# Three later forward transforms at 2.5 classic steps a pair, and 512-token chunks from token 4096, in a fused Fourier-mix and feed-forward kernel

## The chip, the cores and the metric

The kernel runs on one core of a Trainium2 chip. The metric is device time in microseconds (us) of one execution: the median of three runs before is 1351.38 us (1350.46 to 1352.64).

## What is computed

```python
def _attn_ref(x, w_r, w_i, b_r, b_i):            # x: (4, 3008, 256)
    X = np.fft.rfft(x, axis=1)
    Yr = X.real @ w_r - X.imag @ w_i + b_r
    Yi = X.real @ w_i + X.imag @ w_r + b_i
    Yr = np.sign(Yr) * np.maximum(np.abs(Yr) - 0.01, 0.0)
    Yi = np.sign(Yi) * np.maximum(np.abs(Yi) - 0.01, 0.0)
    return np.fft.irfft(Yr + 1j * Yi, n=3008, axis=1)

def _moe_ref(x, w_in, w_out, alpha):             # x: (12032, 256), w_in: (256, 2048)
    h = x @ w_in
    g = np.maximum(h, 0.0) + alpha * np.minimum(h, 0.0)
    return g @ w_out                             # (12032, 256)
```

The first function's result, 4 batches of 3008 tokens, is the second one's input: 12032 tokens. Everything is float32.

## The kernel before

**The transform.** A batch's 3008 points are 47 times 64. Stage a (`a_load`, `a_split`, `a_mm`, `a_evac`, 16 groups a batch) is the 47-point part. Its result goes to DRAM and comes back regrouped as 12 *pairs* (`b_load`). For each pair, stage b (`b_mm`, `b_evac`, `b_evac2`) is the 64-point part; stage m is the complex mix as three real products (`m_mm` two of them, `m_mm2` the third), then the additions, bias and soft shrink on VectorE (`m_part`, in eight parts n = 0 to 7: part 0 adds the bias into a tile Yc, line 526; parts 1 to 4 are four 64-row *quarter additions* from Yc and the third product into a tile Yt, line 532; part 5 bounds, lines 505 and 506; part 6 subtracts, line 511; part 7 makes the low half of a split, line 520); and stage c (`c_mm`, `c_evac`) begins the inverse transform and stores to DRAM. Yt and Yc have one buffer each. Stage d (`d_load`, then `d_step` or `s_dmm`) is the last 47-point part; a call gives 376 tokens, split by `split` (lines 139 and 142) on ScalarE and VectorE into a high and a low half, the feed-forward's input.

**The feed-forward, in two forms.** All its products are of split operands (high times high, high times low, low times high: three matmuls for one).
- *Classic chunks* have 384 tokens (the first of each half of the 16 has 256). A classic *step* is one chunk and one of 16 blocks of 128 hidden units: `l1_step` runs six matmuls into a `ps_h` tile (line 686), ScalarE makes relu(-h) (line 692), VectorE scales and adds (line 693), ScalarE copies the high half gh (line 697), VectorE or GpSimd makes the low half gl (line 698); `l2_step`, three steps later, runs the second layer's matmuls (lines 723 to 725). `CC = 12` chunks are classic, 192 steps in all.
- *512-token chunks* take the rest, from token `T0`. For two hidden blocks at once (a *pair t*, 8 a chunk) `s_l1` runs 12 matmuls (line 791), and `s_sums` and `s_l2` multiply with seven products instead of eight (pair t = 1 is plain, with eight; lines 892 to 894). At a chunk's end `s_out` combines the sums (VectorE, eight operations, lines 920 to 927) and, two pairs later, `s_turn` transposes them (line 936). The last chunk, here called the *rest*, has `ZC` tokens and is plain (`z_parts`, lines 837 and 838; `z_l2`, lines 855 to 857; its copies and stores, lines 862 to 865). `T0` is 4480, so there are 14 full chunks and a rest of 384 tokens.

**What orders the work.** The first batch's transform runs ahead of all this. The three later ones are woven into the classic steps by a table written out by hand: `at(i, fn, ...)` puts a call at the end of step i, and `when=mid` puts it inside step i, between the step's scaling and its gh on the engines' queues. Each engine works in that order. Batch b's pair q has its stage b at step `BO[b] + BP * q`, and its other parts at fixed distances from it: `m_mm` 2 steps later, `m_mm2` 4, the eight parts of `m_part` 3 to 6 (`MP`), `c_mm` 8, `b_load` 4 earlier. Stage a's groups follow `AO[b]`, two in three steps. `d_step` of chunk g of a batch is three steps ahead of its first use.

**Buffers.** The tiles `ps_a`, `ps_b`, `ps_m`, `ps_m1`, `ps_c` and `ps_d` share one PSUM pool of three (`ps_f`), in which the 512-token chunks also hold one accumulator and the rest holds its own. `ps_h` and `ps_o` have two buffers each. DMA: loads and stores go over SyncE's queue (SPq); the last stores alternate over SyncE's and ScalarE's queue (ACTq).

The placing lines:

```python
for q in range(NPAIR if b + 1 < B else 0):
    i = BO[b + 1] + BP * q
    at(i, b_mm, b + 1, q)
    at(i + MM, m_mm, b + 1, q)
    at(i + M2, m_mm2, b + 1, q, when=mid)
    for n, k in enumerate(MP):
        at(i + k, m_part, b + 1, q, n, when=mid)
    at(i + CM, c_mm, b + 1, q)
```

Of the kernel before, what the change touches and what calls it, by code (L numbers as in the profile page):

```python
# [9 lines left out]
F32 = mybir.dt.float32  # L10
# [83 lines left out]
def fft_mix_moe(ctx, tc, x, w_r, w_i, b_r, b_i, w_in, w_out, alpha, la, rb, lc, rd, lf, cf, sel, out):  # L94
    nc = tc.nc
    B, S, C = x.shape
# [10 lines left out]
    TC = 384  # L107
    assert NC * TC - 128 == NC * TOK

    CC = 12  # L110
    SC = 512

    def head(c):
        return 128 - (TC - TOK) * (c % NC) if c % NC else 0

    def size(c):
        return TC if c % NC else TC - 128

    T0 = (CC // NC) * NC * TOK + TC * (CC % NC) - (128 if CC % NC else 0)
    NS2 = -(-(B * S - T0) // SC)  # L120
# [4 lines left out]
    work = ctx.enter_context(tc.tile_pool(name="work", bufs=2))  # L125
# [7 lines left out]
    def f(t):  # L133
        return t.bitcast(F32)
# [275 lines left out]
    bt, xs, xe, yc, ys = {}, {}, {}, {}, {}  # L410
# [94 lines left out]
    def m_bound(t, c):  # L505
        V.tensor_scalar(out=c, in0=t, scalar1=-LAM, scalar2=LAM, op0=ALU.max, op1=ALU.min)

    def m_less(b, q, t, c):
        hi = work.tile([128, 2, C], F32R, tag="Yh", name="Yh")
        lo = work.tile([128, 2, C], F32R, tag="Yl", name="Yl")  # L510
        V.tensor_tensor(out=t, in0=t, in1=c, op=ALU.subtract)
        ys[b, q] = hi, lo, t
# [5 lines left out]
    def m_evac2(b, q):  # L518
        hi, lo, t = ys[b, q]
        V.tensor_tensor(out=lo, in0=t, in1=f(hi), op=ALU.subtract)  # L520

    def m_part(b, q, n):
        if n == 0:
            t = work.tile([128, 2, C], F32, tag="Yt", name="Yt", bufs=1)
            c = work.tile([128, 2, C], F32, tag="Yc", name="Yc", bufs=1)
            V.tensor_tensor(out=c, in0=pm.pop((b, q)), in1=bias[0], op=ALU.add)
            yc[b, q] = t, c
        elif n < 5:

            i, s = divmod(n - 1, 2)  # L530
            t, c = yc[b, q]
            V.tensor_tensor(out=t[64 * i:64 * i + 64, s], in0=p1[b, q][64 * s:64 * s + 64],
                            in1=c[64 * s:64 * s + 64, i], op=ALU.add)
        elif n == 5:
            del p1[b, q]
            m_bound(*yc[b, q])
        elif n == 6:
            m_less(b, q, *yc.pop((b, q)))
        else:
            m_evac2(b, q)  # L540
# [43 lines left out]
    def d_open(c):  # L584
# [3 lines left out]
        if head(c):  # L588
            for t, src in zip((hi, lo), heads.pop(c)):
                if c < CC:  # L590
                    t, src = t[:, :, 0:head(c)], f(src)[:, :, 0:head(c)]
# [8 lines left out]
    def d_step(b, g):  # L600
        t = zt.pop((b, g))
        c = NCH * b + g
        assert c < CC
        n0 = (size(c) - head(c)) // CH
# [20 lines left out]
    def s_open(n):  # L625
        yt[CC + n] = [work.tile([128, CT, SC], F32R, tag=tag, name=tag) for tag in ("yh", "yl")]

# [13 lines left out]
    def s_dpart(dg, n):  # L641
        parts = []
        for k, n0, n1, a, z in s_parts(dg):
            if k == n:
                for ct in range(CT):
                    ps = ds[dg][ct][:, :, n0:n1]
                    ys = [y[:, ct] for y in yt[CC + n]]
                    if n == NS2 - 1:
# [132 lines left out]
    def s_l1(n, t):  # L781
        yh, yl = yt[CC + n]
        w1 = SC if n < NS2 - 1 else ZC
        q = work.tile([128, 2, SC], F32, tag="xt", name="sq")[:, :, 0:w1]
        for j in range(2):
            m = 2 * t + j
            ps = ps_h.tile([128, SC], F32, tag="h", name="ps_h")[:, 0:w1]
            k = 0
            for ct in range(CT):
                for w, a in ((0, yh), (0, yl), (1, yh)):  # L790
                    PE.matmul(ps, wi_h[m // FH][:, w, ct, 128 * (m % FH):128 * (m % FH) + 128], a[:, ct, 0:w1],  # L791
                              start=(k == 0), stop=(k == 3 * CT - 1))
                    k += 1
            A.activation(out=q[:, j], in_=ps, func=AF.Relu, scale=-1.0)  # L794
            V.scalar_tensor_tensor(out=q[:, j], in0=q[:, j], scalar=beta_s[:, m:m + 1], in1=ps,  # L795
                                   op0=ALU.mult, op1=ALU.add)
        sq[n, t] = q
# [160 lines left out]
    ES = [1, 1, 1, 1, 1, 1, 1, 1, 1, 0, 1, 0, 0, 0, 0, 0]  # L958
    LOS = [0, 1, 0, 0, 1, 1, 0, 1, 1, 0, 1, 1, 0, 1, 0, 0, 1, 1, 0, 0, 1, 0, 1, 1, 1, 1, 1, 0, 1, 1, 0, 1, 1, 0, 1, 1, 0, 1, 1, 0, 1, 1, 0, 1, 1, 0, 1, 1]
    DS = 3  # L960
    AO = {2: 58, 3: 95}
    BO = {1: 49, 2: 86, 3: 123}
    BP = 3
    SLAG = 2
    PLAIN = (1,)
    MP = [3, 4, 4, 4, 4, 5, 5, 6]
# [21 lines left out]
    with tc.manual_schedule():  # L988
# [100 lines left out]
        def at(i, fn, *args, when=todo):  # L1089
            when.setdefault(i, []).append((fn, args))  # L1090
# [9 lines left out]
        for b in range(B):  # L1100
            s0 = b * per
            for g in range(J if b == 0 else 0, min(NCH, CC - NCH * b)):
                i = s0 + g * FT
                at(i - 8, d_load, b, g)
                at(i - 4 if i == J * FT else i - FT + 1, d_open, NCH * b + g)
                if b == 0 and g == J:
                    at(i - DS, d_step, b, g)
                else:
                    at(i - 3, d_step, b, g)
            if b == 0:  # L1110
                for g in range(FILL, NG):
                    i = 6 * (g - FILL) + 9
                    if g % 2 == 0:
                        at(i - 8, a_load, 1, g // 2)
                    at(i, a_mm, 1, g)
                    at(i, a_evac, 1, g)
            else:
                for g in range(NG if b + 1 < B else 0):
                    i = AO[b + 1] + 3 * g // 2
                    if g % 2 == 0:  # L1120
                        at(i - 5, a_load, b + 1, g // 2)
                    at(i - 2, a_split, b + 1, g)
                    at(i, a_mm, b + 1, g)
                    at(i, a_evac, b + 1, g)
            for q in range(NPAIR if b + 1 < B else 0):
                i = BO[b + 1] + BP * q
                at(i - BL, b_load, b + 1, q)
                at(i, b_mm, b + 1, q)
                at(i, b_evac, b + 1, q)
                at(i, b_evac2, b + 1, q)  # L1130
# [4 lines that stand above are left out]
                at(i + MP[6], m_evac1, b + 1, q)  # L1135
                at(i + CM, c_mm, b + 1, q)
                at(i + CM, c_evac, b + 1, q)
# [4 lines left out]
        i = NS - 26  # L1142
# [55 lines left out]
        for k in range(len(spairs) + SLAG):  # L1198
# [9 lines left out]
            if k >= SLAG:  # L1208
                n, t = spairs[k - SLAG]
# [43 lines left out]
```

## Time and profile before

| | |
|---|---|
| median of three runs | 1351.38 us (1350.46 to 1352.64) |
| the profiled execution | 1351.47 us |
| its span in the trace | 1349.7 us |
| TensorE busy | 1334.4 us (99%), 9200 matmuls |
| VectorE busy | 1035.8 us (77%) |
| ScalarE busy | 760.9 us (56%) |
| GpSimd busy | 379.0 us (28%) |
| granted TensorE clock | 1.00 (mean of the execution) |

Engines are PE (TensorE; PEld is its weight load), DVE (VectorE), ACT (ScalarE), POOL (GpSimd) and SP (SyncE). A releaser is what ended an engine's idle time. The chain is the run of work that ended last, followed back from the last instruction. The stages of the span: the first batch's transform to about 202 us, classic steps to about 680 us, 512-token chunks to 1311 us, then the rest and the last stores.

### The profile page before, as it was taken

Reading aid. Unit: us, or ns where it says so; the run is one execution under the profiler, and the core shown is the slowest. Engines: PE = TensorE matmul, PEld = TensorE weight load, DVE = VectorE, ACT = ScalarE, POOL = GpSimd, SP = SyncE. Lnnn points to the kernel's source line nnn. Section 1 sums busy time; section 2 is a strip of 40 time slices with the busy share of each in tenths; the row PEclk is TensorE's granted clock in tenths of the full one; section 3 lists DMA queues with packets and bytes.
Section 4 is the critical chain, followed back from the end, with each engine's and each line's share of the span. In section 5 each row is a group of like instructions: output and inputs, shape, how many; then the busy total and the mean of one; then the engine's idle time right before and its main releaser. Section 6 shows DMA issues by size and latency. Waiting matters only on the chain.

```text
span 1349.7 us, 25116 instructions
## 1 busy us (share of the span) xinstructions
PE 1334.4 (99%) x9200; PEld 1250.5 (93%) x9200; DVE 1035.8 (77%) x1934; ACT 760.9 (56%) x1527; POOL 379.0 (28%) x403
## 2 busy tenths in 40 slices
PE   8999999999999999999999999999999999999998
PEld 5979999999999999999999999999999999999998
DVE  2767856776777777776778888888888888888885
ACT  3566655665565555555555555655555556555553
POOL 4854742222221222222121211121112112221222
PEclk9999999999999999999999999999999999999999
DMA  9964223342333312111110110111011101110001
GB/s 244 252 197 136 81 95 105 109 136 72 98 113 114 113 52 79 52 58 41 35 36 2 40 28 5 36 28 28 7 34 28 29 7 34 28 28 9 20 17 28
DMA packets 88117, 89.64 MB, mean 66 GB/s; under 512 B 42317, under 2 KB 70448, under 8 KB 87995
## 3 DMA queue, kind: packets, MB, share of 16 engines
q1 hardware_dynamic: 79700, 77.02, 20.0%
q0 software_dynamic: 5168, 8.02, 2.3%
q10 hardware_dynamic: 3127, 3.01, 0.7%
q8 instruction: 72, 1.18, 0.4%
q14 instruction: 50, 0.41, 0.1%
HBM read 50.49 MB, written 34.34 MB: 63 GB/s over the span
## 4 chain that ended last, share of the span: by engine, by line
PE 90%; DMA 3%; DVE 2%; issue 1%; ACT 1%; SPq 1%; POOL 0%; ACTq 0%; DVEq 0%; POOLq 0%
PE ps_h L791 24%; PE ps_h L686 14%; PE ps_m L488 6%; PE ps_o L893 6%; PE ps_o L894 6%; PE ps_o L892 6%; PE ps_d L617 4%; PE ps_o L725 3%; PE ps_o L724 3%; PE ps_o L723 3%; PE ps_b L428 2%; PE o_last L724 1%; PE o_last L725 1%; PE o_last L723 1%; PE o_last L892 1%; PE o_last L893 1%
## 5 line engine op out<-in xcount | busy, mean ns | idle before, releaser
L791 PE MATMUL ps_h<-yh,w 128*128 128x512 f32 (+1 forms) x960 | 315.6, 390 | 0.0
L830 POOL TENSOR_TENSOR l<-t,h 128x512 fp32r<-128x512 f32 x98 | 127.0, 1296 | 496.5 <-ACT h L828 456.6
L791 PEld LDWEIGHTS ps_h<-yh,w 128*128 128x128 f32 x960 | 180.0, 188 | 33.2
L795 DVE SCALAR_TENSOR_TENSOR sq<-sq,beta_s,ps_h 128x512 f32<-128x512 f32 (+1 forms) x240 | 168.0, 733 | 55.0 <-ACT sq L794 54.2
L686 PE MATMUL ps_h<-yh,w 128*128 128x384 f32 (+1 forms) x704 | 206.8, 336 | 0.9 <-DVE q L693 0.9
L791 PE MATMUL ps_h<-yl,w 128*128 128x512 f32 (+1 forms) x480 | 186.3, 388 | 0.0
L693 DVE SCALAR_TENSOR_TENSOR q<-q,beta_s,ps_h 128x384 f32<-128x384 f32 (+1 forms) x192 | 115.5, 602 | 85.3 <-ACT q L692 83.5
L697 ACT ACTIVATE gh<-q 128x384 fp32r<-128x384 f32 (+1 forms) x192 | 99.1, 516 | 144.5 <-DVE q L693 143.5
L698 POOL TENSOR_TENSOR gl<-q,gh 128x384 fp32r<-128x384 f32 (+1 forms) x90 | 96.6, 1074 | 263.2 <-ACT gh L697 256.4
L810 ACT ACTIVATE dh<-sq 128x768 fp32r<-128x768 f32 x112 | 94.7, 846 | 117.9 <-DVE sq L795 75.2
L794 ACT ACTIVATE sq<-ps_h 128x512 f32<-128x512 f32 (+1 forms) x240 | 133.1, 586 | 27.5 <-PE ps_h L791 23.1
L686 PEld LDWEIGHTS ps_h<-yh,w 128*128 128x128 f32 x704 | 129.4, 189 | 3.8 <-issue 0.8
L828 ACT ACTIVATE h<-t 128x512 fp32r<-128x512 f32 x98 | 62.0, 633 | 105.0 <-DVE t L826 101.7
L686 PE MATMUL ps_h<-yl,w 128*128 128x384 f32 (+1 forms) x352 | 116.5, 331 | 0.0
L692 ACT ACTIVATE q<-ps_h 128x384 f32<-128x384 f32 (+1 forms) x192 | 91.7, 478 | 42.5 <-PE ps_h L686 41.0
L725 PE MATMUL ps_o<-w,gl 128*128 128x256 f32 x384 | 108.0, 281 | 1.7 <-POOL gl L698 1.7
L724 PE MATMUL ps_o<-w,gh 128*128 128x256 f32 x384 | 107.8, 281 | 0.0
L723 PE MATMUL ps_o<-w,gh 128*128 128x256 f32 x384 | 107.7, 281 | 0.0
L791 PEld LDWEIGHTS ps_h<-yl,w 128*128 128x128 f32 x480 | 90.6, 189 | 13.6
L825 DVE TENSOR_TENSOR dl<-sq,dh 128x768 fp32r<-128x768 f32 x98 | 93.5, 954 | 3.8 <-ACT dh L810 3.8
L894 PE MATMUL ps_o<-l,sw_a 128*128 128x256 f32 x294 | 82.0, 279 | 0.0
L892 PE MATMUL ps_o<-h,sw_a 128*128 128x256 f32 x294 | 81.9, 279 | 0.0
(214 smaller groups left out, 3620.2 us busy)
## 6 DMA issues: line engine op xcount, KB each, us to landing
zt<-zd SPq DMA_DIRECT2D x32, 384.0 KB
zd<-zst SPq DMA_DIRECT2D x37, 256.0 KB
ad<-ast SPq DMA_DIRECT2D x48, 192.0 KB
bt<-ad SPq DMA_DIRECT2D x72, 128.0 KB
xt<-in_x SPq DMA_DIRECT2D x21, 320.0 KB
out<-oT SPq DMA_DIRECT2D x152, 32.0 KB
cw_s<-in_moe_w_in SPq DMA_DIRECT2D x8, 512.0 KB
cw_s<-in_moe_w_out SPq DMA_DIRECT2D x8, 512.0 KB
```

Source lines behind the costliest of these rows:

```text
L686: PE.matmul(ps, wi_h[m // FH][:, w, ct, 128 * (m % FH):128 * (m % FH) + 128], a[:, ct, 0:n], start=(k == 0), stop=(k == 3 * CT - 1))
L693: V.scalar_tensor_tensor(out=q, in0=q, scalar=beta_s[:, m:m + 1], in1=ps, op0=ALU.mult, op1=ALU.add)
L697: A.activation(out=hi, in_=q, func=AF.Copy)
L723: PE.matmul(a, hi[:, t], w[:, 0], start=(i, k) in first, stop=False)
L724: PE.matmul(a, hi[:, t], w[:, 1], start=False, stop=False)
L725: PE.matmul(a, lo[:, t], w[:, 0], start=False, stop=(i, k) in last)
L791: PE.matmul(ps, wi_h[m // FH][:, w, ct, 128 * (m % FH):128 * (m % FH) + 128], a[:, ct, 0:w1], start=(k == 0), stop=(k == 3 * CT - 1))
L794: A.activation(out=q[:, j], in_=ps, func=AF.Relu, scale=-1.0)
L795: V.scalar_tensor_tensor(out=q[:, j], in0=q[:, j], scalar=beta_s[:, m:m + 1], in1=ps, op0=ALU.mult, op1=ALU.add)
L830: G.tensor_tensor(out=l24, in0=t24, in1=f(h24), op=ALU.subtract)
L892: PE.matmul(o, wh, gh, start=first, stop=False)
L894: PE.matmul(o, wh, gl, start=False, stop=last)
```

## The change

Three numbers of the order change, and one tile of `m_part` is taken later.

```diff
-    CC = 12
+    CC = 11
...
     def m_part(b, q, n):
         if n == 0:
-            t = work.tile([128, 2, C], F32, tag="Yt", name="Yt", bufs=1)
             c = work.tile([128, 2, C], F32, tag="Yc", name="Yc", bufs=1)
             V.tensor_tensor(out=c, in0=pm.pop((b, q)), in1=bias[0], op=ALU.add)
-            yc[b, q] = t, c
+            yc[b, q] = [c]
         elif n < 5:
 
             i, s = divmod(n - 1, 2)
+            if n == 1:
+                yc[b, q].insert(0, work.tile([128, 2, C], F32, tag="Yt", name="Yt", bufs=1))
             t, c = yc[b, q]
...
-    AO = {2: 58, 3: 95}
-    BO = {1: 49, 2: 86, 3: 123}
-    BP = 3
+    AO = {2: 50, 3: 80}
+    BO = {1: 49, 2: 79, 3: 109}
...
-                i = BO[b + 1] + BP * q
+                i = BO[b + 1] + 5 * q // 2
```

One chunk fewer is classic: 176 classic steps instead of 192. `T0` follows: 4096, with 15 full 512-token chunks instead of 14, and a rest of 256 tokens instead of 384. A transform's pairs are 2 and 3 steps apart in turn (six gaps of 2 and five of 3) instead of 3. From `m_part` on, line numbers are higher by one.

Three places in the engines' orders show what moves. The first is ScalarE in the last transform, near classic step 130: `Xh` is the copy of one pair's stage b, and each `q` and `gh` belong to one classic step. Before:

```order
L442 ACTIVATE Xh<-ps_b 128x2x4x64
L457 ACTIVATE sm<-ps_b 128x2x2x64
L692 ACTIVATE q<-ps_h 128x384
L697 ACTIVATE gh<-q 128x384
L692 ACTIVATE q<-ps_h 128x384
L697 ACTIVATE gh<-q 128x384
L567 ACTIVATE zst<-ps_c 128x512
L516 ACTIVATE Yh<-Yt 128x512
L692 ACTIVATE q<-ps_h 128x384
L697 ACTIVATE gh<-q 128x384
L442 ACTIVATE Xh<-ps_b 128x2x4x64
```

After, between two pairs that are two steps apart:

```order
L442 ACTIVATE Xh<-ps_b 128x2x4x64
L457 ACTIVATE sm<-ps_b 128x2x2x64
L693 ACTIVATE q<-ps_h 128x384
L698 ACTIVATE gh<-q 128x384
L693 ACTIVATE q<-ps_h 128x384
L698 ACTIVATE gh<-q 128x384
L516 ACTIVATE Yh<-Yt 128x512
L442 ACTIVATE Xh<-ps_b 128x2x4x64
```

Between two `Xh` there were three classic steps; here there are two.

The second place is VectorE at the stage-d call for classic chunk 7 (step 109 in both): `yl` and `hl` are the low halves of its split, which read the `ps_d` tiles last; `Yc` and `Yt` are parts of `m_part`. Before:

```order
L693 SCALAR_TENSOR_TENSOR q<-q,beta_s,ps_h 128x384
L506 TENSOR_SCALAR Yc<-Yt 128x512
L511 TENSOR_TENSOR Yt<-Yt,Yc 128x512
L698 TENSOR_TENSOR gl<-q,gh 128x384
L142 TENSOR_TENSOR yl<-ps_d,yh 128x312 x2
L142 TENSOR_TENSOR hl<-ps_d,hh 128x64 x2
L142 TENSOR_TENSOR xl<-xt,xh 94x512
```

After:

```order
L694 SCALAR_TENSOR_TENSOR q<-q,beta_s,ps_h 128x384
L506 TENSOR_SCALAR Yc<-Yt 128x512
L511 TENSOR_TENSOR Yt<-Yt,Yc 128x512
L525 TENSOR_TENSOR Yc<-ps_m,bias 128x512
L699 TENSOR_TENSOR gl<-q,gh 128x384
L142 TENSOR_TENSOR yl<-ps_d,yh 128x312 x2
L142 TENSOR_TENSOR hl<-ps_d,hh 128x64 x2
L448 TENSOR_TENSOR Xl<-ps_b,Xh 128x2x4x64
L458 TENSOR_TENSOR sm<-ps_b,sm 128x2x2x64
```

The next pair's bias addition (line 525) now stands between the subtraction of the pair before it and the splits.

The third place is VectorE at the start of the rest: the last row of `s_out` of the last full chunk, then the rest's first three pairs (`zg` is a low half, line 795 is the scaling), then the first two transposes of `s_turn`. Before:

```order
L927 TENSOR_TENSOR c_16203<-su 128x256
L838 TENSOR_TENSOR zg<-sq,zg 128x384
L795 SCALAR_TENSOR_TENSOR sq<-sq,beta_s,ps_h 128x384 x2
L838 TENSOR_TENSOR zg<-sq,zg 128x384
L795 SCALAR_TENSOR_TENSOR sq<-sq,beta_s,ps_h 128x384 x2
L838 TENSOR_TENSOR zg<-sq,zg 128x384
L936 STREAM_TRANSPOSE oT<-c_16202 128x256
```

After:

```order
L928 TENSOR_TENSOR c_16329<-su 128x256
L839 TENSOR_TENSOR zg<-sq,zg 128x256
L796 SCALAR_TENSOR_TENSOR sq<-sq,beta_s,ps_h 128x256 x2
L839 TENSOR_TENSOR zg<-sq,zg 128x256
L796 SCALAR_TENSOR_TENSOR sq<-sq,beta_s,ps_h 128x256 x2
L839 TENSOR_TENSOR zg<-sq,zg 128x256
L937 STREAM_TRANSPOSE oT<-c_16328 128x256
```

The order is the same; the rest's own rows are 256 columns wide instead of 384, and those of `s_out` and `s_turn` are as they were.

## Rows read from the trace of the kernel before

**Rows 1.** The page: busy time of each engine; the chain's shares by engine.
```profile
PE 1334.4 (99%) x9200; PEld 1250.5 (93%) x9200; DVE 1035.8 (77%) x1934; ACT 760.9 (56%) x1527; POOL 379.0 (28%) x403
...
PE 90%; DMA 3%; DVE 2%; issue 1%; ACT 1%; SPq 1%; POOL 0%; ACTq 0%; DVEq 0%; POOLq 0%
```

**Rows 2.** The waits of PE: tile, line, releaser; total us, count, mean us.
```profile
PE ps_m L488 <- DVE hl L142: 0.5, 1, 0.5
...
PE ps_a L392 <- DVE hl L142: 0.3, 1, 0.3
```

**Rows 3.** Windows: us; PE, PEld, DVE, ACT, POOL busy; PEclk, DMA share, GB/s.
```profile
232.00:328.40 96.40, 96.08 (x700) 92.99 (x699) 73.17 (x140) 59.87 (x124) 24.54 (x31) 1.00 0.36 107
467.70:618.00 150.30, 150.30 (x1150) 150.30 (x1149) 109.03 (x216) 77.29 (x160) 41.00 (x55) 1.00 0.19 61
683.60:1311.00 627.40, 627.40 (x4052) 572.35 (x4051) 538.37 (x1016) 364.78 (x706) 128.91 (x100) 1.00 0.09 24
```

**Rows 4.** The chain in classic steps: start us, us, engine, tile, line, count.
```profile
646.43 1.04 PE ps_h L686 x6
648.54 1.04 PE ps_h L686 x6
```

**Rows 5.** The chain in the first 512-token chunk, first layer of four pairs.
```profile
736.67 2.75 PE ps_h L791 x12
741.90 2.75 PE ps_h L791 x12
747.52 2.75 PE ps_h L791 x12
```

**Rows 6.** The chain in the rest of 384 tokens, two pairs.
```profile
1318.75 0.12 PE ps_o L855
...
1319.11 2.08 PE ps_h L791 x12
...
1323.35 2.08 PE ps_h L791 x12
```

**Rows 7.** Lines by form, DVE: shapes, count, busy us, mean ns, idle before, releaser.
```profile
L693 DVE SCALAR_TENSOR_TENSOR q<-q,beta_s,ps_h 128x384 f32<-128x384 f32 x176 | 107.9, 613 | 82.4 <-ACT q L692 80.7
...
L511 DVE TENSOR_TENSOR Yt<-Yt,Yc 128x512 f32<-128x512 f32 x36 | 25.8, 716 | 1.2
L526 DVE TENSOR_TENSOR Yc<-ps_m,bias 128x512 f32<-128x512 f32 x36 | 24.6, 683 | 0.0
...
L693 DVE SCALAR_TENSOR_TENSOR q<-q,beta_s,ps_h 128x256 f32<-128x256 f32 x16 | 7.6, 475 | 2.8 <-ACT q L692 2.8
```

**Rows 8.** Timeline at the stage-d call of chunk 7: start, us; [idle before, releaser].
```profile
428.49 1.92 PE L617 MATMUL ps_d<-rd_s,zt 96*128 96x94 f32 x16
...
431.31 0.21 DVE L142 TENSOR_TENSOR hl<-ps_d,hh 128x64 fp32r<-128x64 f32 x1
...
431.67 0.71 PE L488 MATMUL ps_m<-ws_s,Xh 128*128 128x256 f32 x4 [0.53 <-DVE hl L142]
```

**Rows 9.** Timeline of DVE in the rest.
```profile
1317.01 0.41 DVE L927 TENSOR_TENSOR c<-su 128x256 f32<-128x256 f32 x1
...
1317.81 1.13 DVE L795 SCALAR_TENSOR_TENSOR sq<-sq,beta_s,ps_h 128x384 f32<-128x384 f32 x2
...
1324.86 1.41 DVE L936 STREAM_TRANSPOSE oT<-c 128x256 f32<-128x256 f32 x4
1326.20 1.09 DVE L795 SCALAR_TENSOR_TENSOR sq<-sq,beta_s,ps_h 128x384 f32<-128x384 f32 x2
```

**Rows 10.** Timeline in a transform: POOL and DVE side by side.
```profile
486.70 0.93 POOL L460 TENSOR_TENSOR Xl<-sm,Xh 128x256 fp32r<-128x256 f32 x1
...
487.06 1.11 DVE L511 TENSOR_TENSOR Yt<-Yt,Yc 128x512 f32<-128x512 f32 x1
```

**Rows 11.** Timeline of the last stores: ScalarE's queue and ScalarE.
```profile
1344.33 1.53 ACTq L336 DMA_DIRECT2D out<-zo  x1
...
1345.91 0.38 ACT L862 ACTIVATE zo<-ps_o 128x256 f32<-128x256 f32 x1 [1.61 <-issue]
```

## The prediction

> **What bounds the kernel now.** I read the page first: TensorE is busy 99% of the span and is 90% of the chain that ended last; VectorE comes next with 77% [rows 1]. So the end is set by the sum of TensorE's work, and anything else counts only where it makes TensorE wait. The second view is therefore the list of TensorE's waits. In the woven transforms it has just two on VectorE, 0.5 and 0.3 us, both for the low half `hl` of a stage-d split, the last reader of a `ps_d` tile [rows 2]. The third view is the table by stretches: in a stretch where two transforms' stages overlap VectorE is busy 73.17 of 96.40 us, in one with pairs alone 109.03 of 150.30, and in the 512-token chunks 538.37 of 627.40, which is 86%, and there TensorE is busy all the time; the granted clock is 1.00, the 2.4 GHz level, in all three [rows 3]. The last view is the chain, which gives the pitch, from start to start, of each kind of step: 2.11 us a classic step [rows 4], 5.23 us a pair of a 512-token chunk and 5.62 us the plain pair [rows 5], 4.24 us a pair of the rest of 384 tokens [rows 6].
>
> The sum is made against the profiled execution, 1351.47 us (span 1349.7, with 1.8 around it). The median of the three runs shown is 0.09 below it. About 0.2% (2.7 us) is what a measurement of this kernel can tell from no change.
>
> **Classic chunk out, 512-token chunk in.** Removed: 16 classic steps, 16 x 2.11 = 33.76 us [rows 4], and the rest of 384 tokens, 8 x 4.24 = 33.92 [rows 6]. Added: one full chunk, 7 x 5.23 + 5.62 = 42.23 [rows 5], and a rest of 256 tokens. That rest has 12 first-layer and 12 second-layer matmuls a pair, all of 256 columns, at 0.12 us each as the second layer shows [rows 6]: 8 x 24 x 0.12 = 23.04. Together 67.68 out and 65.27 in: a gain of 2.4 us. It lies wholly on TensorE, so it counts in full. The transforms' own matmuls, stage d's included, are the same in number and shape; they only stand elsewhere.
>
> **Pairs closer together.** On TensorE nothing is added. What must be shown is that VectorE keeps up. Ahead of it, ScalarE has two classic steps instead of three between two `Xh`, as the order shows, and is the less busy engine. A pair costs VectorE one operation of 683 ns, one of 716 [rows 7] and others that come to some 5.3 us in all (an estimate: bias, subtraction, two low halves at about 0.69 each, four quarters, bound and sum at about 0.42 each). It costs TensorE some 3.8 us (an estimate: 32 matmuls at 0.12). A classic step costs VectorE about 0.9 us: 0.61 for the scaling [rows 7] and a low half in some of the steps. With 7.5 classic steps fewer in the stretch of pairs alone, VectorE's share becomes (109.03 - 7.5 x 0.9) / (150.30 - 7.5 x 2.11) = 76%. Where stages overlap, two more pairs in the same steps make (73.17 + 2 x 5.3) / (96.40 + 2 x 3.8) = 81%. Both are under the 86% at which TensorE does not wait in the 512-token chunks [rows 3], so I take 0 for this. In the three-buffer pool the tile that is taken over was last read by VectorE at least one classic step earlier, at the two-step gaps too; that step, 2.1 us, is the cover. Were it gone, each of the 18 two-step gaps could wait about 0.4 us, as the two waits of rows 2 do. Loads of a pair's data still lead by four steps, and SyncE's and GpSimd's queues carry the same transfers as before, only closer. The later Yt removes an order between two pairs and costs nothing: 0.
>
> **Stage d.** The calls stay at their steps; what stands around them moves. Before, two of them made TensorE wait, 0.8 us in sum [rows 2]. At step 61 the call is now followed by a mix of 12 matmuls before the freed buffer is wanted, so I take its wait as gone. At step 109 the first split's `hl` took until 431.52, and TensorE waited 0.53 for it [rows 8]. Now VectorE has one more bias addition, 683 ns [rows 7], ahead of the splits, as the order shows: 0.53 + 0.68 = 1.2 us. At step 77 a similar crowding gives 0.1. So 1.3 instead of 0.8: a loss of 0.5. Bounds: all waits gone, -0.8; two or three calls at 1.2, +2.5. I take +0.5, since the order there shows one more operation and nothing less.
>
> **The smaller rest.** Its step on TensorE shrinks from 4.24 to 24 x 0.12 = 2.9 us. The work that belongs to the last full chunk does not shrink: eight operations of `s_out` at 0.41, which run up to 1317.42, and four transposes in 1.41 us, both ahead of scalings which free the `ps_h` tiles [rows 9]. Before, the two scalings after `s_out` began at 1317.81, so the first ended at about 1318.4, 0.7 before the first layer that takes its buffer over (1319.11). Those after the transposes began at 1326.20; the first ended at about 1326.8, 0.8 before its first layer (1319.11 + 2 x 4.24 = 1327.59). With 1.4 us less of TensorE's work in a step and 0.14 less in the scaling (475 ns against 613 [rows 7]), the first would wait 1.4 - 0.7 - 0.14, about 0.5, the second about 0.4. Together +0.9. Bounds: 0, where ScalarE and the two `ps_h` buffers take it up, and 2, where neither has a margin and most of 1.26 is waited for twice.
>
> **The end.** The last tile was copied by ScalarE 1.61 us late, behind its own queue's issue of 1.53 [rows 11]. Now there are two tiles, both done at TensorE's end, and one of the two stores goes through ScalarE's queue with that issue of 1.53. What was waited for before is now part of the store: -0.1, bounds -1 and +0.5.
>
> **The sum.** -2.4 + 0 + 0.5 + 0.9 - 0.1 = -1.1 us, from 1351.47 to 1350.4; against the median, a few hundredths of a per cent less than before. I say 1350.4: no change that can be told.
>
> **Rivals.**
> *The waits vanish.* If the order at steps 61 and 109 and in the rest happens to fit, the gain of 2.4 stays and the old 0.8 goes too: 1351.4 - 3.2 = 1348.2 us, faster by just over 0.2%. For it: VectorE has idle time everywhere [rows 3]. Against it: the added operation at step 109 is in the order, and `s_out` does not shrink. Chance 0.15.
>
> *VectorE falls behind in the two-step gaps.* This ends on the other side. In a gap of two steps TensorE has 2 x 2.11 + 3.8 = 8.0 us and VectorE 2 x 0.9 + 5.3 = 7.1, with stage a's split 8.9 against 8.0. So the room is 0.9 us. Operations with both inputs in SBUF are longer while GpSimd works: the subtraction into Yt took 1.11 us beside GpSimd's Xl of 0.93, where the mean of its kind is 0.72 [rows 7, 10]. That is 0.4 more; from three such meetings in a gap on (1.2 over 0.9) VectorE is late, and the next three-step gap must take it up. If one meeting in each of the 18 gaps reaches TensorE, the price is 18 x 0.4 = 7.2, with the gain taken off 1351.4 - 1.1 + 7.2 = 1357.5; if half do, 1354. For it: rows 10. Against it: the mean over 36 such operations is 0.72, so most meet nothing, and at 86% in the 512-token chunks nothing waits [rows 3]. The Trainium skill has a rule for this (SBUF — State Buffer, section "Who interferes with whom"): a VectorE instruction with two SBUF inputs contends with a GpSimd instruction that reads SBUF, and one waits until the other is through, while TensorE and ScalarE never wait. By that rule alone this case would be likelier, as closer pairs bring more meetings; the trace agrees with it at that one place, with 1.11 against 0.72, and shows few such places. Chance 0.17.
>
> *The change does not do what it says.* The order has 15 chunks of 512 tokens and a rest of 256, and pairs two and three steps apart: excluded. A load that comes late on SyncE's queue is what is left of this kind, a chance of 0.02, slower.
>
> **How the numbers follow.** My forecast (between 1348.7 and 1354.1, that is within 0.2%) has 0.66, the first rival 0.15, and the ends on the other side 0.19 together. The likeliest case's own range, by the bounds of the terms, runs from 1351.4 - 2.4 - 0.8 + 0 - 0.5 = 1347.7 to 1351.4 - 2.4 + 2.5 + 2 + 0.5 = 1354.0, with the middle far likelier. The range of 8 in 10 goes from 1348.1, where the waits vanish, to 1354.5, where half of the two-step gaps wait.
>
> **What would show it.** The chain's pitches must stay at 2.11, 5.23 and 5.62, and the pair of the rest must come to 2.9. TensorE's busy time must fall by 2.4 us. The list of TensorE's waits should show `hl` at the call of chunk 7 with about 1.2 us, none at step 61, and waits of the rest's first layer on the scaling of line 796 with 0.9 in sum. The prediction is wrong if TensorE waits at many pairs for Xl, sm, Yt or Yc, if VectorE's share in the transforms goes over 86%, or if the rest's pitch is far from 2.9.

## The result, and the profile after

The changed kernel takes 1365.92 us (median of four runs, 1364.24 to 1367.4) where the kernel before, with the runs beside it, takes 1352.01. The ratio is 1.0104, 95% interval 1.0091 to 1.0116: slower by 1%. The profiled execution took 1364.24 us, its span is 1362.5. Forecast was 1350.4 with a range up to 1354.5.

The page of the changed kernel, engines and the chain's shares:

```profile
PE 1338.0 (98%) x9179; PEld 1246.2 (91%) x9179; DVE 1058.2 (78%) x1979; ACT 758.8 (56%) x1538; POOL 393.8 (29%) x400
...
PE 85%; DVE 7%; ACT 3%; DMA 2%; issue 2%; POOL 1%; SPq 0%; ACTq 0%; DVEq 0%; POOLq 0%
```

TensorE's part of the chain fell from 90% to 85%, and VectorE's and ScalarE's rose from 2% and 1% [rows 1]. So other engines' work now lies on the path. The table by stretches says where. First the kernel before: the classic steps from step 48 on with the three transforms (called the woven part below), the full 512-token chunks, the rest to TensorE's end, and what follows (columns as in [rows 3]):

```profile
201.87:683.69 481.82, 480.85 (x3570) 474.45 (x3569) 349.46 (x678) 270.75 (x566) 124.21 (x162) 1.00 0.27 83
683.69:1305.57 621.88, 621.88 (x4014) 566.83 (x4012) 534.81 (x1010) 361.76 (x701) 126.73 (x98) 1.00 0.10 24
1305.57:1344.60 39.03, 39.03 (x284) 38.82 (x282) 23.52 (x41) 17.80 (x39) 9.57 (x9) 1.00 0.06 15
1344.60:1349.69 5.09, 0.00 (x0) 0.00 (x0) 0.15 (x1) 0.38 (x1) 0.00 (x0) 0.99 0.24 77
```

Then the same four stretches of the changed kernel, and one short piece of its first woven transform (0.54 is the granted clock there):

```profile
202.18:663.08 460.90, 450.24 (x3314) 440.97 (x3313) 337.89 (x649) 246.74 (x528) 133.17 (x153) 1.00 0.27 84
663.08:1328.99 665.91, 665.91 (x4297) 606.89 (x4295) 572.54 (x1082) 386.18 (x749) 134.80 (x104) 1.00 0.10 24
1328.99:1358.25 29.26, 28.81 (x236) 28.10 (x234) 19.38 (x41) 15.13 (x38) 7.49 (x9) 1.00 0.08 19
1358.25:1362.47 4.22, 0.00 (x1) 0.00 (x0) 0.42 (x1) 0.38 (x1) 0.00 (x0) 1.00 0.18 62
239.80:243.50 3.70, 3.70 (x16) 3.66 (x16) 2.62 (x5) 2.41 (x6) 1.11 (x1) 0.54 0.60 156
```

The three stretches behind the woven part took 666.00 us before and 699.39 now: 33.39 more (621.88 to 665.91, 39.03 to 29.26, 5.09 to 4.22). The woven part should have lost more than that: 16 classic steps, 33.76 us by [rows 4], and one stage-d call, 1.92 us by [rows 8], which now belongs to the 512-token chunks; 35.68 in all, so to 446.1 us. It takes 460.90. These 14.8 us are the whole story. TensorE is idle there for 10.7 us (460.90 less 450.24), where it was for 1.0: that is 9.7 of them.

What it waits for, from the list of TensorE's waits of the changed kernel (total us, count, longest):

```profile
PE ps_c L557 <- ACT ast L406: 7.3, 7, 1.9
...
PE ps_c L557 <- DVE Yc L525: 0.9, 2, 0.6
...
PE ps_d L618 <- DVE sm L458: 0.5, 1, 0.5
PE ps_h L792 <- DVE sq L796: 0.5, 1, 0.5
PE ps_b L428 <- PE ps_c L559: 0.4, 1, 0.4
PE ps_a L392 <- DVE sm L458: 0.4, 1, 0.4
PE ps_m L488 <- POOL Xl L460: 0.4, 1, 0.4
```

The line on `ps_h` belongs to the rest, the others to the woven part, whose list names no DMA. None of these stood in the list before, and the two waits on `hl` of [rows 2] are gone. The first line is the main one: seven times stage c's first matmul waits for `ast`, ScalarE's copy of a stage-a result. The timeline at the first of the seven (step 57) shows how that comes about:

```profile
233.80 0.62 DVE L694 SCALAR_TENSOR_TENSOR q<-q,beta_s,ps_h 128x384 f32<-128x384 f32 x1
...
234.78 0.69 DVE L511 TENSOR_TENSOR Yt<-Yt,Yc 128x512 f32<-128x512 f32 x1
...
235.51 0.63 ACT L516 ACTIVATE Yh<-Yt 128x512 fp32r<-128x512 f32 x1 [0.54 <-DVE Yt L511]
...
236.05 0.58 ACT L442 ACTIVATE Xh<-ps_b 128x512 fp32r<-128x512 f32 x1
...
236.66 0.69 DVE L448 TENSOR_TENSOR Xl<-ps_b,Xh 128x512 fp32r<-128x512 f32 x1 [0.71 <-ACT Xh L442]
...
237.44 0.38 ACT L457 ACTIVATE sm<-ps_b 128x256 f32<-128x256 f32 x1 [0.82 <-DVE Xl L448]
237.72 0.58 ACT L406 ACTIVATE ast<-ps_a 96x512 f32<-96x512 f32 x1
...
237.86 0.42 DVE L458 TENSOR_TENSOR sm<-ps_b,sm 128x256 f32<-128x256 f32 x1 [0.51 <-ACT sm L457]
...
238.36 0.38 PE L557 MATMUL ps_c<-Yh,lc_s 128*128 128x256 f32 x1 [1.89 <-ACT ast L406]
```

Read it from the bottom. TensorE starts stage c 0.06 us after `ast` ends; the matmul takes over the buffer that `ast` empties (so the profile puts it, and stage c follows the end of `ast` by 0.05 or 0.06 us at all seven places). `ast` had its input long before (its matmuls ended at 234.3), but on ScalarE's queue it stands behind `sm`; `sm` waits for VectorE's Xl, Xl for ScalarE's `Xh`, and `Xh` stands behind `Yh`, the copy of an earlier pair, which itself waits for VectorE's Yt. That is a chain through two engines that each work in order, and all its links are issued in one step. The same links stand ahead of all seven waits. Stage b's buffer would have been no better: its last reader, VectorE's `sm` (L458), hangs on the same chain and ends within 0.03 us of `ast` each time. `Yh` of pair q is placed 5 steps behind that pair's stage b. With pairs 2 and 3 steps apart in turn, 5 steps is exactly where pair q + 2 has its stage b. Before, with 3 steps, the two never met in a step. Every fifth step has mix, stage b and `Yh` together; in seven of these there is a stage-a group as well, and one step later stage c wants that group's buffer: seven waits.

After the longest of them the granted clock was 0.54 for 3.70 us (the piece above; mostly the lower level, 1.2 GHz), after TensorE had been idle for 1.89 us: 0.46 x 3.70 = 1.7 us more. With the 9.7 us of idle time that makes 11.4 of the 14.8. The other 3.4 lie in TensorE's busy time, and no view here says how they divide; the first matmul of stage c takes 0.38 us after the wait above, where the median of its line is 0.28.

### The profile page after: what moved, and what is told of

Same layout as the page of the kernel before. It is cut to its first block, busy times and chain, and to the rows that moved or that the text cites. A ratio compares the mean times of both kernels' runs of the same rounds, so it can differ in the third digit from the quotient of the medians.

```text
span 1362.5 us, 25205 instructions
## 1 busy us (share of the span) xinstructions
PE 1338.0 (98%) x9179; PEld 1246.2 (91%) x9179; DVE 1058.2 (78%) x1979; ACT 758.8 (56%) x1538; POOL 393.8 (29%) x400
## 4 chain that ended last, share of the span: by engine, by line
PE 85%; DVE 7%; ACT 3%; DMA 2%; issue 2%; POOL 1%; SPq 0%; ACTq 0%; DVEq 0%; POOLq 0%
PE ps_h L792 25%; PE ps_h L687 10%; PE ps_o L894 6%; PE ps_o L895 6%; PE ps_o L893 6%; PE ps_m L488 4%; PE ps_d L618 4%; PE ps_b L428 2%; PE ps_o L726 2%; PE ps_o L725 2%; PE ps_o L724 2%; PE ps_m L475 2%; DVE q L694 2%; PE o_last L893 1%; PE o_last L894 1%
## 5 line engine op out<-in xcount | busy, mean ns | idle before, releaser
L792 PE MATMUL ps_h<-yh,w 128*128 128x512 f32 (+1 forms) x1024 | 332.3, 387 | 0.5 <-DVE sq L796 0.5
L831 POOL TENSOR_TENSOR l<-t,h 128x512 fp32r<-128x512 f32 x105 | 136.1, 1296 | 536.1 <-ACT h L829 473.5
L796 DVE SCALAR_TENSOR_TENSOR sq<-sq,beta_s,ps_h 128x512 f32<-128x512 f32 (+1 forms) x256 | 177.0, 725 | 58.3 <-ACT sq L795 58.0
L792 PE MATMUL ps_h<-yl,w 128*128 128x512 f32 (+1 forms) x512 | 197.1, 385 | 0.0
L687 PE MATMUL ps_h<-yh,w 128*128 128x384 f32 (+1 forms) x640 | 188.1, 337 | 0.9 <-DVE q L694 0.9
L698 ACT ACTIVATE gh<-q 128x384 fp32r<-128x384 f32 (+1 forms) x176 | 90.7, 516 | 152.5 <-DVE q L694 151.3
L694 DVE SCALAR_TENSOR_TENSOR q<-q,beta_s,ps_h 128x384 f32<-128x384 f32 (+1 forms) x176 | 105.5, 600 | 63.4 <-ACT q L693 62.3
L687 PE MATMUL ps_h<-yl,w 128*128 128x384 f32 (+1 forms) x320 | 106.1, 332 | 0.0
L726 PE MATMUL ps_o<-w,gl 128*128 128x256 f32 x352 | 99.1, 281 | 1.7 <-POOL gl L699 1.7
L725 PE MATMUL ps_o<-w,gh 128*128 128x256 f32 x352 | 98.9, 281 | 0.0
L724 PE MATMUL ps_o<-w,gh 128*128 128x256 f32 x352 | 98.8, 281 | 0.0
```

The lines of the kernel that those rows point to most:

```text
L694: V.scalar_tensor_tensor(out=q, in0=q, scalar=beta_s[:, m:m + 1], in1=ps, op0=ALU.mult, op1=ALU.add)
L724: PE.matmul(a, hi[:, t], w[:, 0], start=(i, k) in first, stop=False)
L725: PE.matmul(a, hi[:, t], w[:, 1], start=False, stop=False)
L726: PE.matmul(a, lo[:, t], w[:, 0], start=False, stop=(i, k) in last)
L831: G.tensor_tensor(out=l24, in0=t24, in1=f(h24), op=ALU.subtract)
```

## The experiments

Two theories went to the chip. **Q**: places where ScalarE's and VectorE's queues and the three-buffer pool meet in a bad order; the work of the engines has room. **V**: VectorE cannot keep up with pairs so close, and the waits are only where that shows. Beside the times stands the length of the woven part in each profile, which leaves out what varies at the start of the span: 460.90 us in the changed kernel, 446.1 without loss, and 448.4 (481.82 less 33.39) where the whole kernel would be as fast as before. It is the length in one execution, with what the clock did in it. One spell at the lower level, worth 1.7 us, lies in the woven part of the changed kernel and of experiments 1 to 4 and 10; two, worth 5.1, in that of 8; none in those of 5 to 7, 9, 11 and 12.

**1. The closer pairs alone.**

```diff
-    CC = 11
+    CC = 12
```

> The closer pairs alone, with 12 classic chunks and the rest of 384 tokens as before. Theory Q (closer pairs make the inverse stage's first matmuls wait behind ScalarE's queue, and all of the loss lies in the woven transforms): the chunk exchange gave back about 2 us in the trace (rest and tail included), so this kernel is slower still than the changed one, about 1367 to 1369 us, with the same seven waits of ps_c on the copy ast. Rival X (part of the loss belongs to the exchange of a classic chunk for a 512-token chunk): 1360 us or less.

Measured: 1365.94 us, ratio 1.0115 (1.0096 to 1.0133). The waits and the woven part:

```profile
PE ps_c L557 <- ACT ast L406: 7.3, 7, 1.9
PE ps_c L557 <- DVE Yc L525: 0.9, 2, 0.6
```

```profile
201.31:697.87 496.56, 485.94 (x3570) 476.44 (x3569) 353.86 (x678) 265.47 (x566) 141.09 (x162) 1.00 0.26 79
```

With the same 144 steps as before the woven part is 496.56 instead of 481.82: the closeness alone costs 14.7 us. Against the changed kernel it is 35.66 longer, where the sum says 35.68. X falls; the exchange itself is worth 35.66 - 33.39 = 2.3 us. By the medians this kernel is not told apart from the changed one, so the 2 us that Q named are seen in the stretches only, and the time lies 1 us under Q's range.

**2. Stage a ahead of the mix and stage b in each step.**

```diff
-            for fn, args in when.pop(i, ()):
+            for fn, args in sorted(when.pop(i, ()), key=lambda c: c[0] not in (a_mm, a_evac)):
```

> The changed kernel; in each step stage a's matmuls and their copy go ahead of the mix and of stage b, so ScalarE's queue has ast before Xh and sm. Theory Q: c takes over the buffer of ast a step later, and ast no longer stands behind sm, so the seven waits of 7.3 us in all go, and with the one clock drop about 9 us: 1356 to 1358 us. Rival V (VectorE cannot keep up with pairs this close, and whatever waits is only where it shows): the order on ScalarE changes nothing in VectorE's work, so the waits move and the time stays within 3 us of 1366.

Measured: 1359.56 us, ratio 1.0062 (1.0046 to 1.0079), woven part 457.46. The seven waits are gone, but 1.6 us of `ps_c` on `sm`, 1.4 of `ps_m` on `ast` and 1.3 of `ps_c` on stage a's own matmuls came in. The last is a label: these matmuls had ended 0.6 and 0.8 us before, and VectorE's `sm` ended 0.1 ahead of stage c at both places. So stage c now waits for stage b's buffer, at the end of the same chain. Between the two forecasts, nearer to Q.

**3. Those stage-a groups one step earlier.**

```diff
                     i = AO[b + 1] + 3 * g // 2
+                    i -= i % 5 == 1
```

> The changed kernel; the stage-a groups that fall into the steps in which a mix, a stage b and ScalarE's copy Yh meet (every fifth step) go one step earlier, where neither stands. All work is the same. Theory Q: no ps_c waits on ast any more; 1356 to 1358 us. Rival V: VectorE's work is as dense as before, waits elsewhere, within 3 us of 1366.

Measured: 1357.29 us, ratio 1.0045 (1.003 to 1.006), woven part 454.90. Waits:

```profile
PE ps_a L392 <- DVE sm L458: 1.8, 3, 0.9
PE ps_c L557 <- DVE Yc L525: 0.9, 2, 0.6
PE ps_m L488 <- POOL Xl L460: 0.6, 2, 0.4
```

As Q said: moving eight groups by one step (those of the seven waits, and that of step 51), with VectorE's work as it was, takes 8.6 us off by the medians, 6.0 of them seen in the woven parts of the two profiles, and no wait on `ast` is left there. This is the run that tells Q from V for the seven waits.

**4. Stage c one step later.**

```diff
-    CM = 8
+    CM = 9
```

> The changed kernel; stage c of every pair one step later (nine steps behind stage b instead of eight). Theory Q: c no longer comes straight after the step with ast, so the seven waits go, unless another buffer's reader stands there in its place: 1356 to 1359 us. Rival V: within 3 us of 1366, since VectorE's queue is as it was.

Measured: 1366.54 us, ratio 1.0112 (1.0097 to 1.0127), woven part 462.72. Q missed here. The waits:

```profile
PE ps_a L392 <- ACT ast L406: 5.1, 4, 1.9
PE ps_a L392 <- ACT zst L568: 2.8, 3, 1.0
PE ps_c L557 <- DVE Yt L533: 2.6, 2, 1.7
```

The late `ast` stayed late, and the next taker of its buffer, now a stage-a group, waited for it instead. The delay sits in the release of the buffer; moving one taker only changes who waits. By itself this run would have spoken for V.

**5. ScalarE's `Yh` behind `Xh`, `sm` and `ast`.**

```diff
-            for fn, args in when.pop(i, ()):
+            for fn, args in sorted(when.pop(i, ()), key=lambda c: c[0] is m_evac1):
```

> The changed kernel; ScalarE's copy Yh of an earlier pair goes behind the copies Xh, sm and ast where they meet in a step, instead of ahead of them. Theory Q (ScalarE's queue delays the reader that frees c's buffer: Yh waits for VectorE, and Xh, sm and ast wait behind it): ast ends about 0.6 to 1.2 us earlier at each of the seven places, so the waits of 7.3 us fall to 1 to 3 and the time to 1358 to 1362 us. Rival V (VectorE's queue itself is late there, whatever ScalarE's order): Xl and sm stay as late as they are, the waits stay at about 7, and the time within 2 us of 1366.

Measured: 1359.49 us, ratio 1.0056 (1.0039 to 1.0072), woven part 456.88. `ast` is now waited for 4.3 us in five places instead of 7.3 in seven: the time is in Q's range, the waits fell by less than it said. ScalarE's order was part of the chain; Xl behind Yt on VectorE is another part, and stays.

**6 to 8. Stage d out of the dense steps too.** The stage-d calls go to the step of each five that has no mix and no stage b or c; experiment 7 adds the order of 5, and experiment 8 a new pattern for stage a.

```diff
-                at(i - 8, d_load, b, g)
+                at(i - 8 - (i - 3) % 5, d_load, b, g)
...
-                    at(i - 3, d_step, b, g)
+                    at(i - 3 - (i - 3) % 5, d_step, b, g)
...
+                    i -= i % 5 == 1
```

> As e3_a_elsewhere, and the stage-d calls moved up to the step of each five in which neither a mix nor stages b or c are issued (1 to 4 steps earlier; their loads too). Theory Q, as a matter of the three-buffer pool: a stage-d call takes two of the three buffers for the time of its splits, and beside a mix and a stage b it is the rest of the loss; the waits at steps 61, 77, 93 and 109 (about 4 us of waiting with a clock drop) go: 1352 to 1354 us. Rival V: VectorE's work is unchanged, so the waits come back elsewhere and the time stays at 1356 or more.

> As e6_a_and_d, with ScalarE's Yh behind Xh, sm and ast too. Theory Q: 0 to 1.5 us below e6, 1351 to 1353 us. Rival V: no difference from e6.

> As e7, with stage a's groups in a pattern of four in five steps, two in the step without mix, b and c, and one in each of the two steps before it, instead of ten in fifteen; stage a is over sooner. Theory Q: the last waits of stage a's tile for sm (1.8 us in e3) go, 1350 to 1352 us. Rival V: more stage-a splits in a stretch make VectorE denser there, so it is slower than e7 by 1 us or more.

Measured: 6: 1355.66 us, ratio 1.0028 (1.0018 to 1.0038), woven part 451.84. 7: 1355.62 us, 1.0028 (1.0018 to 1.0038), 452.19. 8: 1357.23 us, 1.0039 (1.0023 to 1.0054), 455.64. The largest wait of 7 is

```profile
PE ps_a L392 <- DVE Yt L533: 2.3, 2, 1.1
```

In 6, the waits at the moved calls went (`ps_d` on `sm` and `ps_c` on Yc are not in its list) and the woven part lost another 3.1 us (1.7 of them the spell at the lower clock that 3's profile has and 6's has not), but the median stayed 1.7 above what Q gave, and 7 is no better than 6. The reason is in the row: in steps 60 and 90 a stage-a group stands in the step to which stage d was moved, behind its two buffers. Experiment 8 put two groups there: 2.9 us in this wait, and 0.9 in waits of the second group on `hl`. By its time it did as V said. But in its profile the clock fell after both places, once for 3.4 us (254.6 to 258.0) and once for longer:

```profile
380.90:387.70 6.80, 6.60 (x22) 5.30 (x22) 2.78 (x8) 2.57 (x6) 0.08 (x1) 0.50 0.33 95
```

Half of these 10.2 us, 5.1, is lost to the clock, which is more than the 3.45 that its woven part is longer than 7's. Three of its four runs have a mean granted clock of 0.996; the one at 1.000 took 1354.92 us, less than the median of 7. So its loss is of those two places and of the clock after them, and it does not tell Q from V.

**9. Stage a ahead of stage d there.**

```diff
-            for fn, args in sorted(when.pop(i, ()), key=lambda c: c[0] is m_evac1):
+            for fn, args in sorted(when.pop(i, ()), key=lambda c: (c[0] is d_step) + 2 * (c[0] is m_evac1)):
```

> As e7_a_d_copy, but where a stage-a group and a stage-d call fall into one step (steps 60 and 90), stage a goes first. Theory Q: the waits of ps_a on the quarter additions Yt there (2.3 us in e7) shrink to about 0.5 on ps_d, so 1353 to 1354.5 us. Rival V: VectorE's split is as late, no change from e7 (1355.6).

Measured: 1352.94 us, ratio 1.0011 (1.0001 to 1.002). Waits and woven part:

```profile
PE ps_m L488 <- ACT zst L568: 1.2, 3, 0.5
PE ps_a L392 <- DVE sm L458: 0.9, 2, 0.6
PE ps_a L392 <- ACT zst L568: 0.3, 1, 0.3
```

```profile
203.98:653.80 449.82, 447.47 (x3315) 438.40 (x3314) 342.25 (x649) 245.41 (x528) 120.51 (x153) 1.00 0.28 86
```

The order of two calls in two steps took 2.4 us off. With the pairs as close as in the change, 11.1 of the 14.8 us are back by order alone (460.90 to 449.82), 1.7 of them by the clock, which did not fall in this woven part.

**10. Less work for VectorE.**

```diff
-        (V if LOS[(2 * m + c) % len(LOS)] and fill or not fill and (m + c) % 2 else G).tensor_tensor(
+        (V if LOS[(2 * m + c) % len(LOS)] and fill or not fill and (m + c) % 2 and not J <= c < 9 else G).tensor_tensor(
```

> As e7_a_d_copy, with the classic low halves gl of chunks 3 to 8 all on GpSimd instead of half of them on VectorE, which takes some 0.55 us off VectorE in every other step. Rival V (VectorE is too late): most of what e7 still loses goes, 1351 to 1353 us. Theory Q (few places, by order of queues and buffers): within 1.5 us of e7. Rival C (GpSimd's work lengthens VectorE's operations): slower than e7 by 2 us or more.

Measured: 1355.37 us, ratio 1.0028 (1.0017 to 1.004), woven part:

```profile
203.49:656.22 452.73, 448.43 (x3314) 439.64 (x3313) 319.99 (x601) 247.31 (x528) 174.27 (x201) 1.00 0.28 85
```

VectorE has 320 us of work in the woven part instead of 342 (experiment 7), GpSimd 174 instead of 120, and the time is that of 7. The clock fell once in this woven part and not in 7's; without those 1.7 us it would be 451.0, 1.2 less than 7's 452.19. So VectorE's load is worth about 1 of the 6 us that 7 still loses, not most of them: V falls, and so does C. The run stands on the order of 7, where the seven waits are gone; for the changed kernel itself, experiment 3 is the test.

**11 and 12. As close as needed, and no closer.** The first of the three transforms keeps 3 steps a pair; the other two have 2.5. The stage-d calls and stage a avoid the meeting steps in the second; calls in one step go in the order of 9. 12 also moves the stage-d calls of chunks 4 and 5 one step later (`i - 2` for the last `i - 3` of the diff).

```diff
-    AO = {2: 50, 3: 80}
-    BO = {1: 49, 2: 79, 3: 109}
+    AO = {2: 58, 3: 86}
+    BO = {1: 49, 2: 85, 3: 115}
...
-                    at(i - 3, d_step, b, g)
+                    j = i - 3 - (i - 4) % 5 if i > 88 else i - 3
+                    at(j, d_step, b, g)
...
+                    i -= b == 2 and i % 5 == 2
...
-                i = BO[b + 1] + 5 * q // 2
+                i = BO[b + 1] + (5 * q // 2 if b else 3 * q)
```

> The exchange of the chunk with as little closeness as it allows: the first of the three transforms at 3 steps a pair as before, the other two at 2.5, starting at steps 85 and 115; stage-d calls of the dense stretch in the step without mix, b and c, stage a out of the step with mix and b, ScalarE's Yh last. Theory Q: the first transform loses nothing again and the second about 2 to 3 us, so 1350 to 1352.5 us, no slower than before. Rival V: the loss goes by VectorE's density, which is lower in a third of the stretch only: 1353 us or more.

> As e11_mixed, with the stage-d calls of chunks 4 and 5 one step later, which puts that of chunk 4 into a step (62) without mix, b and c. Theory Q: the wait of 0.9 us of ps_m on Yc and what goes with it at step 61 goes: about 1 us below e11 in the woven part, 1350.5 us, with the ratio to before between 0.998 and 1.000. Rival V: no difference from e11.

Measured: 11: 1351.73 us, ratio 1.0003 (0.9994 to 1.0013). 12: 1351.4 us beside 1351.55 of before, ratio 0.9995 (0.9986 to 1.0004). Woven parts of 11 and 12:

```profile
201.41:650.00 448.59, 446.69 (x3315) 438.62 (x3313) 341.05 (x649) 247.42 (x528) 119.44 (x153) 1.00 0.28 87
```

```profile
202.84:650.97 448.13, 446.60 (x3315) 438.67 (x3313) 340.95 (x649) 247.13 (x528) 119.21 (x153) 1.00 0.28 87
```

Both have the exchanged chunk and are as fast as the kernel before, as 448.4 for the break-even says. Of the 2.3 us that the exchange brings, some 2 are still lost in the woven part; idle time shows 0.6 of them in 12 (1.5 us, 448.13 less 446.60, against 1.0 before). Neither beats the kernel before by more than the measurement's uncertainty; 12 against 11 is not settled by the times, and by the woven part it is 0.5 us. The forecast for 12 named the wrong wait: the 0.9 us of `ps_m` on Yc stand in both lists (at 399.4 and 400.4 us), and what went is a wait of 0.7 of `ps_d` on `ast`.

## Why the prediction was wrong

**The step that failed** is "Pairs closer together", with "so I take 0 for this" and its reason: "In the three-buffer pool the tile that is taken over was last read by VectorE at least one classic step earlier, at the two-step gaps too; that step, 2.1 us, is the cover." Two things in it were wrong. It looked at VectorE's readers alone, and the buffer that stage c takes over was last read by ScalarE's `ast`. And it took a step of TensorE's time for the cover, as if the reader ran when its place in the order comes. In truth the reader stood behind four links on two in-order queues, and ended up to 1.9 us after TensorE wanted the buffer. The term was 0; the closer pairs, with stage d's crowding in it, cost 14.7 us (experiment 1), and moving the stage-a groups out of the way gave 6.0 to 8.6 back (experiment 3). The order rows ahead of the prediction showed only gaps without a stage-a copy; in the overlapped stretch, which no place covered, `Yh`, `Xh`, `sm` and `ast` stand in one step. The price named for a lost cover, about 0.4 us at 18 gaps, comes to 7.2 us, close to the 7.3 of the waits on `ast`; that is luck, since these are seven places of 0.4 to 1.9 us, and half of the whole loss.

**The shares of engines were no proof.** The estimates of 76% and 81% for VectorE against 86% in the 512-token chunks were near enough: over the woven part it is 337.89 of 460.90, 73%. A share below another stage's share says that the work fits, not that the release of a buffer comes in time. Experiment 10 shows the other half, on the order of 7: with 22 us less of VectorE's work about 1 us came back.

**The rival on the slow side had the right sign and the wrong mechanism.** It had VectorE falling behind through GpSimd. The subtraction into Yt became shorter, not longer, than its mean of 716 ns [rows 7] (shortest, median and longest of the 36, in ns):

```profile
L511 DVE TENSOR_TENSOR Yt<-Yt,Yc x36: 691/693/694, 225.3 to 583.6; 128x512 f32<-128x512 f32 x36
```

None of them comes near the 1.11 us of [rows 10]. The rule that stood beside it (the Trainium skill, SBUF — State Buffer, section "Who interferes with whom": a VectorE operation with two SBUF inputs contends with a GpSimd operation that reads SBUF) may hold at single places, as [rows 10] shows; here the low half Yl (L520) is the one with long cases, up to 1.02 us against a median of 0.69. But no such long operation stands in the chains ahead of the seven waits, so it had no part in them.

**Stage d.** Forecast was one wait of 1.2 us on `hl` at step 109, 0.1 at step 77, none at step 61, and a loss of 0.5 in all. Step 61 came as forecast. The added bias operation is there, but what TensorE waits for first is that operation itself (from the timeline of step 109):

```profile
465.21 0.69 DVE L525 TENSOR_TENSOR Yc<-ps_m,bias 128x512 f32<-128x512 f32 x1
...
465.96 0.39 PE L557 MATMUL ps_c<-Yh,lc_s 128*128 128x256 f32 x1 [0.32 <-DVE Yc L525]
...
467.07 0.21 DVE L142 TENSOR_TENSOR hl<-ps_d,hh 128x64 fp32r<-128x64 f32 x1
...
467.38 1.13 PE L428 MATMUL ps_b<-rb_s,bt 128*128 128x128 f32 x8 [0.45 <-PE ps_c L559]
```

The second wait, 0.45, is put down to TensorE's own stage c, which had ended 0.45 us before. The first `hl` ends at 467.28, 0.1 ahead of stage b, and frees the first `ps_d` tile; the other two buffers of the pool are still being read then. So the forecast wait on `hl` most likely came, at 0.45 instead of 1.2.

The term was right that stage d would be crowded, and too small: TensorE waits 0.8 us there and 1.0 at the call of step 77 (0.45 for its second `ps_d` tile and 0.58 ahead of stage c), 1.8 in all against a forecast of 1.3. Moving the calls and ordering them took 5 us off (454.90 in experiment 3 to 449.82 in 9, with `Yh` last in it), 1.7 of them the clock's. It was costed by one call and one reader; the other calls meet mixes and stages b and c at other places of the five-step pattern.

**The chunk exchange** was right. Forecast 2.4 us; in the stretches it is 2.3, with the 1.1 that the rest loses and the 0.9 that the end gives back (both below), so 2.5 without them. The pitches stayed, as the chain of the changed kernel shows for two pairs of a 512-token chunk and two of the rest:

```profile
705.62 2.75 PE ps_h L792 x12
...
710.85 2.75 PE ps_h L792 x12
...
1349.62 1.44 PE ps_h L792 x12
...
1352.50 1.44 PE ps_h L792 x12
```

5.23 as before [rows 5], and 2.88 for the rest.

**The smaller rest** was right too: TensorE's matmuls fell by 33.92 - 23.04 = 10.9 us, the stretch by 39.03 - 29.26 = 9.8, so 1.1 is lost, where +0.9 was forecast. The chain shows its larger part where it was expected, behind `s_out`:

```profile
1339.40 0.33 DVE c L928
1339.74 0.33 DVE zg L839
1340.07 0.40 DVE sq L796
...
1340.52 1.69 PE ps_h L792 x12
...
1346.53 1.65 PE ps_h L792 x12
```

The wait itself is 0.5 us, as the list has it, and this first layer takes 1.69 where 1.44 is usual. Behind the transposes, the second place named, 1.65 is all that shows: 0.2 where 0.4 was forecast. Another 1.64, at 1333.1 us and ahead of `s_out`, was not forecast; with these three the 1.1 is complete.

**The end** gave back more than forecast: 5.09 to 4.22, so -0.9 instead of -0.1, which fits ScalarE's queue: its issue there took 0.67 us (at 1359.16) and not the 1.53 of [rows 11].

**The signs named in advance** told right: "TensorE waits at many pairs for Xl, sm, Yt or Yc" came closest, with `ast` as the name that was not on the list. That TensorE's busy time would fall by 2.4 us did not come: it rose from 1334.4 to 1338.0, by 1.7 us since matmuls ran at the lower clock after a wait; the rest is not accounted for.

**The range.** Its lower end by the bounds of the terms took -0.5 for the end of the kernel, where that term's own bound was -1; 1347.2 would follow instead of 1347.7. The miss was on the other side and does not hang on it.

## What to carry to other kernels

For a buffer that is taken over, follow its last reader back through the queues of *all* engines in their order, to the first link that waits; a step of the bound engine is a cover only if that chain is shorter. When work on a hand-made order gets a new period, look which distances of the table become multiples of it: here a distance of 5 met a period of 5, and operations that never shared a step began to share one in every five. If a wait moves when its waiter is moved (experiment 4), move the release instead (experiments 3 and 5).

## What the runs showed that was not expected

The exact same first part, up to step 48, ends between 200.24 us (experiment 7) and 203.98 (experiment 9, with a spell of the lower clock worth 1.7 in it) of the span in these profiles, a spread larger than the gain looked for; only the stretches told effects of 1 to 3 us apart. And an idle time of 1.89 us of TensorE was followed by 3.70 us at a granted clock of 0.54, so that a single wait cost nearly twice its length. The length of a wait does not tell whether the clock falls: in experiment 3 it fell (to 0.50, from 324.8 us on) after waits of 0.44 and 0.58 at 322.4 and 324.0, while the changed kernel has the same two waits (0.45 and 0.58, at 327.4 and 329.1) and no fall behind them. The stretches of two profiles are therefore compared with the clock beside them.
